# Attention and two mixtures in one kernel: the shifted copy of v made by DMA, and the first expert's weight splits moved off GpSimd

## The chip, the core and the metric

One core of a Trainium2 chip runs the whole program. The metric is the device time of one execution in microseconds (us). Before the change three runs took 689.7, 691.38 and 685.89 us; their median is 689.7 us. One further execution was profiled, and all rows below come from it; its span is 693.8 us. The engines are TensorE (PE; PEld is its weight load), VectorE (DVE), ScalarE (ACT), GpSimd (POOL) and SyncE (SP), which in this program issues the transfers.

## What is computed

Three stages follow each other: windowed attention, a dense mixture of 4 experts over all tokens, and a routed mixture of 8 experts. Only the first two matter for the change.

```python
# attention: q, k, v of (2, 8, 576, 64); a query sees the 64 positions up to its own
scores = scale * np.matmul(q, k.transpose(0, 1, 3, 2))
mask = (rel >= 0) & (rel < window)
attn = softmax(np.where(mask, scores, -1e9))
x = np.matmul(attn, v)              # becomes 1152 tokens of 512
# dense mixture, 4 experts
for e in range(E):
    h = np.maximum(x @ w1[e], 0.0)  # 512 -> 1024
    out += p[:, e:e + 1] * (h @ w2[e])
# routed mixture, 8 experts, one for each token: follows on out
```

## The kernel before, in words

**Precision.** Every large product is made of three matmuls: each operand is split in a high part (a rounded copy) and a low part (the rest). A piece of expert weights is loaded as 512 KB into one of four `raw` buffers (`w_load`, L317 for w1, L319 for w2). `w_split` then makes the high part (L333, a cast) and the low part (L337, a subtraction). Each of w1 and w2 of an expert has four such pieces, c = 0 to 3. A `raw` buffer is free for the next load when the low part of its piece is done.

**Attention.** There are 18 units u of 64 queries, two in each tile t of 128 tokens. `at_s` makes a unit's scores (PE, L415), their maximum (DVE, L428 and L429), the exponentials (ACT, L435), the reciprocal of the sum (DVE, L442 and L443) and the normalised weights `s` (POOL, L446). `at_pv` transposes `s` (PE, L365), copies it out of PSUM to `pT` (ACT, L458; 2 buffers), multiplies with v (PE, L465, "PV" below; one `o` buffer in PSUM) and splits the result into `xth` (ACT, L473) and `xtl` (DVE, L474). The keys of a unit are 128 tokens. For an odd unit they are the tile's own `vn`. For an even unit they are the first half of this tile and the second half of the tile before: the shifted copy `ve` (`mk_ve`, L395 and L398; 2 buffers, while `vn` has 3). The queries and keys are transposed by `at_q` and `at_k` (PE, L365).

**Dense mixture.** `gemm1_chunk` (L525) makes 128 columns of h for a group of tokens; group 0 of the first expert holds 256 tokens and needs `xth` and `xtl` of units 0 to 3 and all of w1. `gemm2_tile` (L546) needs w2. PE may start on these while attention is still going on, and does so.

**Order.** The program is written as operations with an engine, a planned duration, what they read and write, and a priority. A list scheduler (`Plan.run`) turns them into one fixed order for each engine before anything runs; each engine then works through its list and stops at the first instruction whose inputs are missing. SP has such a list too: a `dma_start` that has to wait holds back all transfers behind it. The table `KN` holds priorities and choices: `w1pool`, `w1hpool` and `w2pool` say for each of the four pieces of the first expert whether POOL makes the low part of w1, the high part of w1 and the low part of w2.

Of the kernel before, what the change touches and what calls it, by code (L numbers as in the profile page):

```python
# [15 lines left out]
PSUM = bass.MemoryType.PSUM  # L16
# [13 lines left out]
RP, RH = ((1, 3), (2, 1), (2, 3)), ((1, 2), (2, 2))  # L30
KN = {'mpe': [1, 1, 1, 1, 1, 1, 1, 0, 0, 0, 0, 0, 0, 0, 0, 0, 0, 0], 'UT': 37.5, 'ULATE': -12.9, 'w1p': [3.5, 16.0, 16.5, 20.5], 'w1pool': [1, 0, 0, 0], 'w1hpool': [1, 0, 0, 1], 'ld': [-20.0, -15.9, 3.5, 0.0, -0.9, 4.0], 'w1ld': [-12.5, 2.4, 7.3, 6.7], 'ldb': 0.3, 'lds': 2.4, 'ldv': 65.5, 'qd': [0, 1, 1, 0, 1, 0, 1, 1, 0], 'w2p': 37.8, 'w2s': 18.7, 'w2pool': [1, 1, 0, 0], 'sl': 0.4, 'oq': -38.3, 'ok': -29.0, 'ove': -5.4, 'opv': -6.5, 'dpp': 22.8, 'wpool': [0, 0, 0, 0, 0, 0, 0, 0]}
NU = NT // 64
KC = DM // 128
# [16 lines left out]

# [1 line left out]
class Ring:  # L52
    """a tile tag with n buffers"""

# [11 lines left out]
class Buf:  # L66
    """one use of a ring's buffer; it gets its tile when its first op is emitted"""

# [25 lines left out]
class Plan:  # L94
# [6 lines left out]
    def add(self, eng, dur, fn, rd=(), wr=(), prio=0.0, new=None, slack=0.0):  # L101
        """fn emits; rd and wr are keys (or Bufs) read and written; new: Bufs that get their tile here"""
        o = Op()
        o.slack = slack
        o.eng, o.dur, o.fn, o.prio, o.seq, o.acq = eng, dur, fn, prio, len(self.ops), list(new or ())
        wr = list(wr) + o.acq
        deps = set()
        for x in rd:
            if x in self.w:
                deps.add(self.w[x])  # L110
        for x in wr:
            if x in self.w:
                deps.add(self.w[x])
            deps.update(self.r.get(x, ()))
        for x in rd:
            self.r.setdefault(x, []).append(o)
        for x in wr:
            self.w[x] = o
            self.r[x] = []
        deps.discard(o)  # L120
        o.deps, o.outs, o.wait = deps, [], len(deps)
        for d in deps:
            d.outs.append(o)
        o.bufs = [x for x in dict.fromkeys(list(rd) + wr) if isinstance(x, Buf)]
        for x in o.bufs:
            x.left += 1
        self.ops.append(o)
        return o
# [78 lines left out]
def fused_kernel(ctx: ExitStack, tc: tile.TileContext, q, k, v, dp, w1, w2, wskip, wgate, m1, m2, out):  # L207
# [58 lines left out]
    add = plan.add  # L266

# [1 line left out]
    def c_ident():  # L269
# [26 lines left out]
    def warm(i):  # L296
# [5 lines left out]
        rd=["ident"], wr=["psum1"], prio=-9)  # L302
# [7 lines left out]

# [1 line left out]
    def w_load(src, part, c, prio, extra=False, early=False):  # L312
# [35 lines left out]

# [1 line left out]
    qn, kn, vn, ve, su = {}, {}, {}, {}, {}  # L350
# [41 lines left out]
    def mk_ve(t, pr):  # L392
        w, a = ve_r.buf(), vn[t]
        ve[t] = w
        add("DVE", 0.33, lambda: DVE.tensor_copy(w[0:64], a[0:64]), rd=[a], new=[w], prio=pr)  # L395
        if t:
            c = vn[t - 1]
            add("DVE", 0.33, lambda: DVE.tensor_copy(w[64:128], c[64:128]), rd=[c], wr=[w], prio=pr)  # L398
            c.close()
        else:  # L400
            add("POOL", 0.46, lambda: POOL.memset(w[64:128], 0.0), wr=[w], prio=pr)
# [108 lines left out]

# [1 line left out]
    seq = [0]  # L512
# [49 lines left out]

# [1 line left out]
    R = {"rpr": Ring(None, 3, [128, 128], F32, "rp")}  # L564
# [62 lines left out]
    def route(t):  # L627
# [108 lines left out]
        def spread(c0, c1, pr, after=()):  # L736
            """columns c0 to c1 of w (0, 1: the token's number; 2 to 4: its gate) to the table of slots"""
            e0, n = c0 * E2, (c1 - c0) * E2
# [85 lines left out]

# [1 line left out]
    rings = [{}, wa]  # L826
# [41 lines left out]
    def xsplit(ps, pr):  # L868
        """ps: PSUM buffers that hold KC chunks between them"""
        x, w = M["xs"].buf(), KC // len(ps)  # L870
# [12 lines left out]
    def block(e, j, xg, x, small=False):  # L883
        """up to 128 rows of one expert; small: up to 64 rows, high and low parts side by side in one stationary"""
        ring, key = rings[e], rkey[e % 2]
# [7 lines left out]
        def gemm(name, ps, c, groups, g0=0, g1=None):  # L893
            """groups: list of (operand, its keys, weights, chunks, column slice)"""
            for n, (op, keys, ws, ks, cols) in list(enumerate(groups))[g0:g1]:
# [89 lines left out]

# [1 line left out]
    npass = [0]  # L987
# [19 lines left out]
    with tc.manual_schedule():  # L1007
# [47 lines left out]
        def over(e, i):  # L1055
            """more than 64 * i rows for expert e"""
            return (nv[0] & (7 * 8 ** e)) > (i - 1) * 8 ** e

        def tail(e, j, xt):
            """expert e's rows from 128 * j on, of which there is at least one"""  # L1060
            x = xgs[e, j]
# [93 lines left out]
```

## Time and profile before

| | before |
|---|---|
| runs, median (lowest to highest) | 689.7 us (685.89 to 691.38) |
| span of the profiled execution | 693.8 us |
| PE busy | 641.8 us (93%) |
| DVE busy | 343.1 us (49%) |
| ACT busy | 225.7 us (33%) |
| POOL busy | 140.2 us (20%) |
| mean granted TensorE clock | 0.961 |

Busy time is the union of an engine's instructions; a share of the whole span is a mean over stages that have different limits. Attention takes about the first 95 us, the dense mixture lasts to about 480 us, the routed one to the end. The granted clock 1.00 is 2.4 GHz, 0.50 is 1.2 GHz. The profiled execution is 4.1 us longer than the median of the runs.

### The profile page before, as it was taken

The page shows a single profiled execution, that of the slowest core. Times are in us where ns is not written, and L with a number is a line of the kernel's source. Part 1 is how long each engine was busy: PE and PEld are TensorE (multiplying, and loading weights), DVE is VectorE, ACT ScalarE, POOL GpSimd, SP SyncE. Part 2 cuts the span into 40 slices and gives each one's busy share as a digit, 9 for nine tenths or more (in the row PEclk, how much of TensorE's full clock was granted, in tenths as well). Part 3 has the DMA queues.
Part 4 walks back from the last instruction along what each step waited for, and adds up shares of the span by engine and source line. Part 5 has one row for each costly group of instructions (what it writes and reads, how often), then busy time and mean ns, then how long its engine had stood idle before and what let it go on. Part 6 is the DMA issues. An engine that isn't in the chain of part 4 may idle for free. (4 is left out here: it accounts for less than half of the span.)

```text
span 693.8 us, 9629 instructions
## 1 busy us (share of the span) xinstructions
PE 641.8 (93%) x3652; PEld 563.5 (81%) x3652; DVE 343.1 (49%) x688; ACT 225.7 (33%) x480; POOL 140.2 (20%) x129
## 2 busy tenths in 40 slices
PE   6889999999999999999999999999879888999754
PEld 5788899898989989898989898898758666778543
DVE  5996922147212144121244262657457648937931
ACT  4964731035101133110134121135216524525500
POOL 6550320000000000000000000006047617625610
PEclk9999999999999999999999999999689989999977
DMA  9767000019000034000034110117176664853500
GB/s 216 154 166 225 17 3 1 0 47 296 22 1 1 0 98 146 0 1 1 1 121 122 43 49 32 61 50 265 61 251 224 219 229 131 282 189 101 183 19 12
DMA packets 55372, 70.13 MB, mean 101 GB/s; under 512 B 32857, under 2 KB 32857, under 8 KB 55296
## 3 DMA queue, kind: packets, MB, share of 16 engines
q1 hardware_dynamic: 52912, 62.17, 28.9%
q0 software_dynamic: 2384, 6.97, 3.4%
q8 instruction: 44, 0.72, 0.4%
q14 instruction: 32, 0.26, 0.1%
HBM read 62.43 MB, written 7.47 MB: 101 GB/s over the span
## 5 line engine op out<-in xcount | busy, mean ns | idle before, releaser
L525 PE MATMUL mm<-xth,wa1h 128*128 128x384 f32 (+1 forms) x416 | 137.8, 331 | 0.0
L525 PE MATMUL mm<-xtl,wa1h 128*128 128x384 f32 (+1 forms) x416 | 135.7, 326 | 0.0
L525 PE MATMUL mm<-xth,wa1l 128*128 128x384 f32 (+1 forms) x416 | 135.7, 326 | 0.0
L531 ACT ACTIVATE hh<-mm 128x384 fp32r<-128x384 f32 (+1 forms) x104 | 48.5, 466 | 235.7 <-PE mm L525 227.1
L546 PE MATMUL mm<-wa2h,hh 128*128 128x512 f32 (+1 forms) x296 | 117.2, 396 | 0.0
L533 DVE SCALAR_TENSOR_TENSOR hl<-mm,hh 128x384 fp32r<-128x384 f32 (+1 forms) x104 | 54.5, 525 | 122.9 <-ACT hh L531 122.9
L546 PE MATMUL mm<-wa2h,hl 128*128 128x512 f32 (+1 forms) x296 | 115.0, 388 | 0.0
L546 PE MATMUL mm<-wa2l,hh 128*128 128x512 f32 (+1 forms) x296 | 115.0, 388 | 0.0
L525 PEld LDWEIGHTS mm<-xth,wa1h 128*128 128x128 f32 x416 | 78.7, 189 | 0.7
L525 PEld LDWEIGHTS mm<-xtl,wa1h 128*128 128x128 f32 x416 | 78.7, 189 | 0.5
L525 PEld LDWEIGHTS mm<-xth,wa1l 128*128 128x128 f32 x416 | 78.6, 189 | 0.0
L768 POOL DMA_INDIRECT x<-scr,id x1 | 1.3, 1252 | 360.2 <-DVE id L785 360.2
L546 PEld LDWEIGHTS mm<-wa2h,hl 128*128 128x128 f32 x296 | 55.8, 188 | 12.4
L558 DVE SCALAR_TENSOR_TENSOR x<-mm,prob,x 128x512 f32<-128x512 f32 (+1 forms) x28 | 20.5, 731 | 91.2 <-PE mm L546 91.2
L546 PEld LDWEIGHTS mm<-wa2l,hh 128*128 128x128 f32 x296 | 56.0, 189 | 11.0
L546 PEld LDWEIGHTS mm<-wa2h,hh 128*128 128x128 f32 x296 | 55.9, 189 | 11.1
L337 DVE TENSOR_TENSOR wa2l<-raw,wa2h 128x1024 fp32r<-128x1024 f32 x22 | 40.2, 1837 | 4.9 <-ACT wa2h L333 4.7
L333 ACT CAST wa2h<-raw 128x1024 fp32r<-128x1024 f32 x29 | 30.3, 1047 | 21.8 <-PE mm L546 19.4
L333 ACT CAST wa1h<-raw 128x1024 fp32r<-128x1024 f32 x27 | 27.0, 1049 | 22.5 <-PEq L1109 11.0
L337 DVE TENSOR_TENSOR wa1l<-raw,wa1h 128x1024 fp32r<-128x1024 f32 x25 | 31.6, 1306 | 1.3 <-ACT wa1h L333 1.1
L899 PE MATMUL mm<-wb1h,xs 128*128 128x512 f32 x64 | 25.1, 466 | 7.7 <-PEq L1109 6.8
L947 DVE SCALAR_TENSOR_TENSOR ht<-pt,ht 128x512 fp32r<-128x512 f32 (+2 forms) x27 | 15.1, 567 | 32.8 <-ACT ht L944 31.2
(209 smaller groups left out, 1003.9 us busy)
## 6 DMA issues: line engine op xcount, KB each, us to landing
raw<-in_moe_w_dram SPq DMA_DIRECT2D x96, 512.0 KB, 5.0
scr<-x SPq DMA_DIRECT2D x9, 256.0 KB, 2.1
out_dram<-x SPq DMA_DIRECT2D x9, 256.0 KB, 2.3
qn<-in_q_dram SPq DMA_DIRECT2D x8, 256.0 KB, 4.6
kn<-in_k_dram SPq DMA_DIRECT2D x8, 256.0 KB, 4.1
vn<-in_v_dram SPq DMA_DIRECT2D x8, 256.0 KB, 4.8
qn<-in_q_dram SPq DMA_DIRECT2D x2, 128.0 KB, 4.6
kn<-in_k_dram SPq DMA_DIRECT2D x2, 128.0 KB, 4.7
```

The lines of the kernel that those rows point to most:

```text
L333: (POOL.tensor_copy if hpool else DVE.tensor_copy if hdve else ACT.copy)(out=aps()[0], in_=b.tile)
L337: (POOL if pool else DVE).tensor_tensor(out=l, in0=b.tile, in1=f32(h), op=ALU.subtract)
L525: PE.matmul(out=ps[:, 0:n], lhsT=wa[a][:, kk, f * 128:(f + 1) * 128], rhs=x[:, kk, g0:g0 + n], start=(i == 0), stop=(i == 3 * KC - 1))
L531: add("ACT", c_act(n), lambda: ACT.activation(out=hh[:, f, 0:n], in_=ps[:, 0:n], func=ACTF.Relu), rd=[ps], wr=[("hh", f)], prio=-1)
L533: add("DVE", c_dve(n), lambda: DVE.scalar_tensor_tensor(out=hl[:, f, 0:n], in0=ps[:, 0:n], scalar=0.0, in1=f32(hh[:, f, 0:n]), op0=ALU.max ...
L546: PE.matmul(out=ps[:, 0:c1 - c0], lhsT=x[:, f, o:o + 128], rhs=wa[a][:, f, c0:c1], start=(f == 0 and i == 0), stop=(f == FC - 1 and i == 2))
L558: DVE.scalar_tensor_tensor(out=z, in0=y, scalar=prob[:, t, e:e + 1], in1=z, op0=ALU.mult, op1=ALU.add)
L768: add("POOL", 1.0, lambda: POOL.indirect_dma_start(out=R["x0"], out_offset=None, in_=scr[0:128 * (GT + 1), :], in_offset=bass.IndirectOffs ...
L899: PE.matmul(out=ps[:, 0:cols.stop - cols.start], lhsT=op(k), rhs=ring[f"{c}{a}"][:, k, cols], start=(n == 0 and k == ks[0] and a == "h"), ...
L947: add("DVE", c_dve(w * n), lambda: DVE.scalar_tensor_tensor(out=ht[:, s, n:2 * n], in0=p[:, 0:w, 0:n], scalar=0.0, in1=f32(ht[:, s, 0:n]), ...
```

## The change

Two things are edited. The entries `w1pool`, `w1hpool` and `w2pool` of the first expert become all zero: the high parts of w1's pieces 0 and 3 go from POOL to ACT, the low part of piece 0 of w1 and of pieces 0 and 1 of w2 from POOL to DVE. And `mk_ve` copies the two halves of `ve` by `dma_start` on SP, from SBUF to SBUF, where DVE copied before: 9 copies at L395 and 8 at L398, each of 64 partitions by 512 values (128 KB). The rest of the diff takes comments away.

```diff
-KN = {'mpe': [1, 1, 1, 1, 1, 1, 1, 0, 0, 0, 0, 0, 0, 0, 0, 0, 0, 0], 'UT': 37.5, 'ULATE': -12.9, 'w1p': [3.5, 16.0, 16.5, 20.5], 'w1pool': [1, 0, 0, 0], 'w1hpool': [1, 0, 0, 1], 'ld': [-20.0, -15.9, 3.5, 0.0, -0.9, 4.0], 'w1ld': [-12.5, 2.4, 7.3, 6.7], 'ldb': 0.3, 'lds': 2.4, 'ldv': 65.5, 'qd': [0, 1, 1, 0, 1, 0, 1, 1, 0], 'w2p': 37.8, 'w2s': 18.7, 'w2pool': [1, 1, 0, 0], 'sl': 0.4, 'oq': -38.3, 'ok': -29.0, 'ove': -5.4, 'opv': -6.5, 'dpp': 22.8, 'wpool': [0, 0, 0, 0, 0, 0, 0, 0]}
+KN = {'mpe': [1, 1, 1, 1, 1, 1, 1, 0, 0, 0, 0, 0, 0, 0, 0, 0, 0, 0], 'UT': 37.5, 'ULATE': -12.9, 'w1p': [3.5, 16.0, 16.5, 20.5], 'w1pool': [0, 0, 0, 0], 'w1hpool': [0, 0, 0, 0], 'ld': [-20.0, -15.9, 3.5, 0.0, -0.9, 4.0], 'w1ld': [-12.5, 2.4, 7.3, 6.7], 'ldb': 0.3, 'lds': 2.4, 'ldv': 65.5, 'qd': [0, 1, 1, 0, 1, 0, 1, 1, 0], 'w2p': 37.8, 'w2s': 18.7, 'w2pool': [0, 0, 0, 0], 'sl': 0.4, 'oq': -38.3, 'ok': -29.0, 'ove': -5.4, 'opv': -6.5, 'dpp': 22.8, 'wpool': [0, 0, 0, 0, 0, 0, 0, 0]}
...
     def mk_ve(t, pr):
         w, a = ve_r.buf(), vn[t]
         ve[t] = w
-        add("DVE", 0.33, lambda: DVE.tensor_copy(w[0:64], a[0:64]), rd=[a], new=[w], prio=pr)
+        add("SP", 0.4, lambda: SP.dma_start(out=w[0:64], in_=a[0:64]), rd=[a], new=[w], prio=pr)
         if t:
             c = vn[t - 1]
-            add("DVE", 0.33, lambda: DVE.tensor_copy(w[64:128], c[64:128]), rd=[c], wr=[w], prio=pr)
+            add("SP", 0.4, lambda: SP.dma_start(out=w[64:128], in_=c[64:128]), rd=[c], wr=[w], prio=pr)
             c.close()
```

Since the scheduler plans with other engines and durations, it writes another order for attention on every engine. Three places are shown. The number behind a name tells the buffers apart; in brackets stands what an instruction waits for (DMAHW0 to DMAHW7 are the counters that SP's transfers use in turn).

SP, from the load of q's tile 7 on. Before (`qn_534` is q's tile 7, `raw_584` the first piece of w2, `vn_631` v's tile 2):

```order
L354 DMA qn_534<-in_q_dram 128x8x64 [waits DMAHW2_49,PE_49]
L354 DMA kn_547<-in_k_dram 128x8x64 [waits DMAHW3_49,PE_49]
L507 DMA prob_100<-in_moe_domain_probs_dram 128x9x4 [waits DMAHW0_49]
L319 DMA raw_584<-in_moe_w2_dram 128x2x512 [waits DMAHW1_49,Pool_49]
L319 DMA raw_608<-in_moe_w2_dram 128x2x512 [waits DVE_49]
L354 DMA vn_631<-in_v_dram 128x8x64
L354 DMA vn_655<-in_v_dram 128x8x64 [waits DMAHW4_49,DVE_49]
L319 DMA raw_676<-in_moe_w2_dram 128x2x512 [waits DMAHW5_49,DVE_49]
```

And now (`qn_504` is q's tile 7, `raw_525`, `raw_540`, `raw_551` and `raw_556` are the four pieces of w2, `vn_284`, `vn_306` and `vn_546` v's tiles 0 to 2, `ve_554` the shifted copy for unit 2, `ve_559` that for unit 4, `raw_562` the first piece of the second expert's w1):

```order
L354 DMA qn_504<-in_q_dram 128x8x64 [waits DMAHW3_49,PE_49]
L507 DMA prob_100<-in_moe_domain_probs_dram 128x9x4
L319 DMA raw_525<-in_moe_w2_dram 128x2x512 [waits DMAHW1_49,DVE_49]
L319 DMA raw_540<-in_moe_w2_dram 128x2x512 [waits DMAHW2_49,DVE_49]
L354 DMA vn_546<-in_v_dram 128x8x64
L319 DMA raw_551<-in_moe_w2_dram 128x2x512 [waits DMAHW4_49,DVE_49]
L395 DMA ve_554<-vn_306 64x512 [waits DMAHW5_49]
L319 DMA raw_556<-in_moe_w2_dram 128x2x512 [waits DMAHW6_49,DVE_49]
L395 DMA ve_559<-vn_546 64x512 [waits DMAHW7_49,DMAHW3_49,Pool_49]
L317 DMA raw_562<-in_moe_w1_dram 128x1024 [waits DMAHW1_49,DMAHW0_49,DVE_49]
L398 DMA ve_554<-vn_284 64x512
```

The second half of unit 2's copy now stands on SP behind `ve_559`, which waits for v's tile 2 to land, and behind `raw_562`, which takes the buffer of `raw_525` and so waits until DVE has made the low part of that piece.

PE, from the transposes of unit 4 to the first matmul of the dense mixture. Before (`sp_465` and `sp_499` are the scores of units 8 and 9, `o_477` is the PV of unit 3, `qn_449` q's tile 5, `kn_462` k's tile 5; the PV of units 0 and 2 are done by then):

```order
L365 MATMUL pt_457<-ident_93,s_364 128x128 x4
L415 MATMUL sp_465<-kt0_114,qz0_112 128x128 x4
L465 MATMUL o_477<-pT_453,vn_310 64x64 x8
L365 MATMUL pt_493<-ident_93,qn_449 128x128 x4
L415 MATMUL sp_499<-kt0_114,qz0_112 128x128 x4
L365 MATMUL pt_509<-ident_93,kn_462 128x128 x4
L525 MATMUL mm_519<-xth_106,wa1h_108 128x256
```

And now (`s_363`, `s_393`, `s_451` and `s_456` are units 4 to 7, `sp_466` and `sp_474` the scores of units 8 and 9, `o_442`, `o_569` and `o_590` the PV of units 3, 2 and 5, `qn_432` is q's tile 5):

```order
L365 MATMUL pt_436<-ident_93,s_363 128x128 x4
L465 MATMUL o_442<-pT_420,vn_306 64x64 x8
L365 MATMUL pt_460<-ident_93,s_393 128x128 x4
L415 MATMUL sp_466<-kt0_114,qz0_112 128x128 x4
L415 MATMUL sp_474<-kt0_114,qz0_112 128x128 x4
L365 MATMUL pt_493<-ident_93,qn_432 128x128 x4
L365 MATMUL pt_513<-ident_93,s_451 128x128 x4
L465 MATMUL o_569<-pT_355,ve_554 64x64 x8
L365 MATMUL pt_583<-ident_93,s_456 128x128 x4
L465 MATMUL o_590<-pT_580,vn_546 64x64 x8
L525 MATMUL mm_601<-xth_106,wa1h_108 128x256
```

The PV of unit 2, with its shifted copy `ve_554`, has moved behind q's tile 5. Ahead of the dense mixture there now stand three more transposes (units 5, 6 and 7) and one more PV (unit 5), and k's tile 5 comes later; ahead of q's tile 5 there stand one more unit's scores and one more transpose, and one PV fewer.

ACT, behind the exponentials of unit 9 (`s_518` is unit 9; `pt_460` is the transposed unit 5, `o_569` the result of unit 2's PV). Before, ACT's casts of w2 stood one at a time between outputs of the dense mixture (L531):

```order
L333 CAST wa2h_110<-raw_584 128x1024 [waits DMAHW1_49]
L531 ACTIVATE hh_104<-mm_612 128x256 [waits PE_49]
L333 CAST wa2h_110<-raw_608 128x1024 [waits DMAHW2_49]
L531 ACTIVATE hh_104<-mm_635 128x256 [waits PE_49]
L531 ACTIVATE hh_104<-mm_657 128x256 [waits PE_49]
```

And now:

```order
L435 ACTIVATE s_518,mx_527<-s_518,mx_527 128x128 x3
L333 CAST wa2h_110<-raw_525 128x1024 [waits DMAHW1_49]
L333 CAST wa2h_110<-raw_540 128x1024 [waits DMAHW2_49]
L333 CAST wa2h_110<-raw_551 128x1024 [waits DMAHW4_49]
L333 CAST wa2h_110<-raw_556 128x1024 [waits DMAHW6_49]
L458 COPY pT_580<-pt_460 128x512 [waits PE_49]
L473 CAST xth_106<-o_569 128x4x64
```

All four casts of w2 now stand together, ahead of unit 5's `pT` and unit 2's `xth`. On DVE the four low parts of w2 (L337) stand together in the same way, ahead of unit 2's `xtl`.

## Rows read from the trace of the kernel before

**Rows 1.** Busy time by stretch; columns: stretch, length, busy of each engine, clock, DMA, GB/s.
```profile
20.00:30.00 10.00, 7.90 (x94) 6.92 (x94) 8.84 (x24) 8.68 (x40) 5.52 (x6) 1.00 0.78 196
30.00:34.16 4.16, 3.81 (x45) 3.65 (x45) 4.09 (x8) 3.95 (x13) 1.04 (x1) 1.00 0.10 23
34.16:50.70 16.54, 14.29 (x131) 13.78 (x129) 15.63 (x38) 11.88 (x39) 7.82 (x5) 1.00 0.68 166
50.70:480.00 429.30, 429.23 (x2472) 386.36 (x2473) 170.90 (x414) 114.37 (x241) 20.29 (x40) 1.00 0.20 63
```

**Rows 2.** Instructions in order of time: the one long PE wait; columns: start, length, instruction.
```profile
43.26 4.74 POOL L337 TENSOR_TENSOR wa2l<-raw,wa2h 128x1024 fp32r<-128x1024 f32 x2
45.92 2.36 DVE L395 COPY ve<-vn 64x512 f32<-64x512 f32 x1
50.71 0.51 PE L465 MATMUL o<-pT,ve 128*64 128x64 f32 x10 [2.26 <-DVE xtl L474]
```

**Rows 3.** Busy time in two stretches at half clock, columns as in rows 1.
```profile
52.06:55.40 3.34, 3.34 (x17) 3.28 (x16) 2.38 (x5) 1.25 (x6) 0.00 (x0) 0.50 1.07 318
514.80:519.70 4.90, 4.88 (x12) 3.88 (x13) 0.00 (x0) 0.00 (x0) 0.00 (x0) 0.50 0.98 306
```

**Rows 4.** Instructions of PE in order of time, 30 to 34.2 us.
```profile
30.35 0.63 PE L365 MATMUL pt<-ident,s 128*128 128x128 f32 x4 [1.47 <-ACT pT L458]
30.82 1.06 PE L415 MATMUL sp<-kt,qz 128*128 128x128 f32 x8
31.80 0.68 PE L465 MATMUL o<-pT,vn 128*64 128x64 f32 x16
32.42 0.66 PE L365 MATMUL pt<-ident,qn 128*128 128x128 f32 x4
...
33.80 0.60 PE L365 MATMUL pt<-ident,kn 128*128 128x128 f32 x4
34.16 0.36 PE L525 MATMUL mm<-xth,wa1h 128*128 128x256 f32 x1
```

**Rows 5.** Transfers that SP issues, in order of time; columns: start, length of issue, transfer.
```profile
33.10 0.37 SPq L354 DMA_DIRECT2D qn<-in_q_dram  x1
34.43 0.37 SPq L354 DMA_DIRECT2D kn<-in_k_dram  x1
34.85 0.58 SPq L507 DMA_DIRECT2D prob<-in_moe_domain_probs_dram  x1
35.52 1.51 SPq L319 DMA_DIRECT2D raw<-in_moe_w_dram  x2
```

**Rows 6.** Issues with KB and us to landing, at 34.85, 35.52, 37.08, 38.27; last: whole span.
```profile
prob<-in_moe_domain_probs_dram SPq DMA_DIRECT2D x1, 18.0 KB, 3.2
raw<-in_moe_w_dram SPq DMA_DIRECT2D x1, 512.0 KB, 4.2
vn<-in_v_dram SPq DMA_DIRECT2D x1, 256.0 KB, 5.3
raw<-in_moe_w_dram SPq DMA_DIRECT2D x1, 512.0 KB, 6.6
scr<-x SPq DMA_DIRECT2D x9, 256.0 KB, 2.1
```

**Rows 7.** Groups of instructions, 0 to 100 us; columns: busy us, mean ns, idle before.
```profile
L333 ACT CAST wa2h<-raw 128x1024 fp32r<-128x1024 f32 x4 | 4.2, 1038 | 0.0
L337 DVE TENSOR_TENSOR wa2l<-raw,wa2h 128x1024 fp32r<-128x1024 f32 x2 | 2.4, 1224 | 0.1
L398 DVE COPY ve<-vn 64x512 f32<-64x512 f32 x8 | 3.4, 424 | 0.2
L458 ACT COPY pT<-pt 128x512 f32<-128x512 f32 x18 | 10.6, 587 | 3.8 <-PE o L465 2.8 <-PE pt L365 0.8
L473 ACT CAST xth<-o 128x256 fp32r<-128x256 f32 x18 | 6.7, 371 | 5.8 <-PE o L465 5.7
L474 DVE TENSOR_TENSOR xtl<-o,xth 128x256 fp32r<-128x256 f32 x18 | 7.5, 415 | 1.5 <-ACT xth L473 1.4
```

## Prediction

> **What bounds the kernel now.** I read the busy time by stretch first. From 50.7 us to 480 us PE is busy for 429.23 of 429.30 us, in the three stretches from 20 us up to there it is idle for 2.10, 0.35 and 2.25 us, and the first matmul of the dense mixture starts at 34.16 us [rows 1]. So until 480 us PE does its list without a gap, and whatever PE loses in the first 50 us comes out at the end one for one. Attention decides how much that is: DVE is busy for 8.84 of 10 us, 4.09 of 4.16 and 15.63 of 16.54 us in the three stretches from 20 us on [rows 1], ahead of PE in none of them by much, and the order on each engine is fixed.
>
> Next I looked for PE's idle time in the timeline. The 2.25 us of the stretch from 34.16 us are one wait of 2.26 us for unit 5's `xtl` [rows 2]. On DVE that `xtl` stood behind copies of `ve`, one of which took 2.36 us while POOL was making two low parts of w2 for 4.74 us [rows 2]; the second copies are 0.42 us long on average [rows 7]. A little after this idle time the granted clock fell to 0.50, that is 1.2 GHz, from 52.06 to 55.40 us, PE busy all along [rows 3]: 3.34 us in which half the work was done, 1.67 us lost. The change removes just these two things, the copies from DVE and the splits from POOL. At most 2.25 + 1.67 = 3.9 us are to be had from it there.
>
> Then I read how SP behaves. q's tile 7 was issued at 33.10 us, when PE had finished transposing tile 5 (32.42 + 0.66) [rows 4, 5]. k's tile 7 came at 34.43 us, right after PE had transposed k's tile 5 (33.80 + 0.60) [rows 4, 5], and `prob` and two pieces of w2 followed at 34.85 and 35.52 us [rows 5], though nothing that they need was late. A transfer that waits on SP holds back those behind it.
>
> **The change part by part.** *Removed from DVE*: 17 copies of some 0.42 us [rows 7], 7 us over attention. *Added to DVE*: three low parts at 1.22 us [rows 7], 3.7 us. *Added to ACT*: two casts of about 1.04 us [rows 7]. In sum DVE has 3 us less to do; it is not what I expect to end last, so I price these at nothing apart from the 3.9 us above. The first cast and low part of w1 fall in the first 10 us, where ACT and DVE wait for PE in any case; if that cover failed it would cost 1 to 2 us.
>
> *The 17 copies on SP, and the new order.* Let t0 be the moment when q's tile 5 has been transposed; 33.08 us before. By the order printed above PE now has one more unit's scores (0.98 us from row to row), one more transpose (0.47) and one PV fewer (0.62) ahead of it [rows 4]: 0.83 us more, t0 = 33.9, if PE's idle time up to there stays; 31.5 if all 2.45 us of idle between 20 and 34.16 us [rows 1] vanish with the lighter DVE. DVE has only 0.8 to 1.2 us less to do up to there (two or three copies), so I take 33.4.
>
> From t0 on, with the spacing of issues seen before (0.42 us behind q or k, 0.67 behind `prob`, 0.75 for a piece of w2 [rows 5]; for v and a half of `ve` I estimate 0.4 to 0.5 from the 0.37 of q): `prob` at t0 + 0.4, w2's pieces 0 and 1 at + 1.1 and + 1.9, v's tile 2 at + 2.6, piece 2 at + 3.1, the first half of `ve_554` at + 3.9, piece 3 at + 4.3. Now `ve_559` waits for v's tile 2: 2.6 + 5.3 [rows 6] = 7.9. Behind it `raw_562` waits for the low part of piece 0: landed at 1.1 + 4.2 [rows 6] = 5.3, cast 1.04 and low part 1.22 [rows 7], 7.6. So `raw_562` is issued at t0 + 8.3 and the second half of `ve_554` only at t0 + 9.1.
>
> How long a copy within SBUF takes no row shows. From below: a 256 KB store that has the queue to itself lands after 2.1 us [rows 6]; t0 + 11.2. From above: it lands behind everything ahead of it. Piece 3 lands by 4.3 + 6.6 = 10.9, and `raw_562` 4.2 to about 6 us [rows 6] after its issue; t0 + 12.5 to 14.5. `prob`, with its 18 KB, took 3.2 us behind k's tile, longer than the 256 KB store alone [rows 6]; so I lean to the upper end and take t0 + 13. The Trainium skill's page "DMA: Bandwidth & Descriptors", section "Queues, rings and completion order", says that each DMA engine consumes the descriptors of one queue in ring order, though a later one may complete earlier. By that rule the copy starts behind `raw_562` and the sum is the one taken; with the 2.1 us alone it would be 1.8 us less. The row on `prob` agrees with it.
>
> The PV of unit 2 starts then, and nothing on PE's list can be done meanwhile but one transpose. Behind it: PV 0.68 us [rows 4], `pT` of unit 5 0.59, `xth` 0.37, `xtl` 0.42 [rows 7], the PV of unit 5 0.68, some 0.4 us for five hand-overs (an estimate from the gaps between such rows): 3.1 us. The dense mixture starts at t0 + 16.1 = 49.5 us.
>
> The same start is held back a second time. ACT has all four casts of w2 ahead of that `pT` and `xth`, and DVE all four low parts ahead of `xtl`. Piece 3 lands at t0 + 10.9; cast 1.04, low part 1.22, `xtl` 0.42, the PV of unit 5 0.68: t0 + 14.3 with no copy late at all. If `ve` came in time, this would be late next.
>
> **The sum**, against the profiled execution. The start of the dense mixture moves from 34.16 to 49.5 us, 15.3 us. Of that, three transposes and a PV less k's transpose (3 x 0.47 + 0.62 - 0.4, about 1.6 us [rows 4]) are work that PE no longer has to do later: 13.7 us lost. The old wait and its slow clock are given back: -3.9. A PE idle for over 10 us comes back at half clock: after the idle time ahead of 514.80 us it was at 0.50 for 4.90 us [rows 3], so +2.4. Behind that PE has some 40 us of work in attention and group 0 and DVE some 30, so I add 1 us of further waits (0 to 4): each v tile has to wait for a `ve` half to land before its buffer is free, and each `ve` for a v tile. 13.7 - 3.9 + 2.4 + 1 = 13.2 us: 707.0 us for a profiled execution like this one, which lies 4.1 us above the median of the runs; against the median 689.7, **702.9 us**. Low end: t0 = 31.5, copy at + 11.2, no further waits: 8.5 us, 698.2. High end: t0 = 33.9, copy at + 14.5, 4 us of waits: 18.2 us, 707.9.
>
> **The rivals.** *Faster: the copies arrive in time.* If SP reached the second half of `ve_554` before PE needs it, and w2 landed before ACT needs it, PE would keep its 34 us start and the 3.9 us would be won: 685.8 us. The copy of 2.36 us beside POOL's 4.74 us [rows 2] speaks for it; so does the Trainium skill's page "SBUF — State Buffer", section "Who interferes with whom": VectorE and GpSimd share a port pair as an exclusive lock, the later one blocks. The length of the copy agrees: it ended with POOL's work. Against it stands the order on SP and ACT. It decides from a start of the dense mixture at about 38 us on: 4 us late, less 1.6 us of work moved, plus 1.2 to 2.4 us of slow clock, eat the 3.9. I see no way to load, cast and split four pieces between 33.4 and 38 us. 5 in 100.
>
> *Held back but not long.* If w2's pieces landed after 4.2 us each rather than 6.6, and the copy after 2.1, and t0 was 31.5, the start would be at 43 to 44 us: 6 to 7 us lost net, 696 us, about within 1%. The rows of 5.3 and 6.6 us, from just this place in the program [rows 6], speak against it. 10 in 100.
>
> *Attention goes on at the pace of SP.* Each later tile needs v (5.3 us), then `ve` (2.1 to 4 us), before the buffer of v is free for the next but two. If PE waited for that at units 6, 8 and 10, 2 us each, or at more, the time would be 709 to 713 us. By my reckoning PE is about 1 us behind the copies there. 12 in 100.
>
> **How the numbers follow.** The likeliest case, 73 in 100, gives 702.9 with 698 to 708. To leave out no more than 2 in 10 the range reaches from 696.5 to 709. A measurement of this kernel tells about 1% from no change, 682.8 to 696.6: faster 0.04, same 0.09, slower 0.87.
>
> **What would show it.** In the profile after: the first L525 at 46 to 51 us instead of 34.16; ahead of it a PE wait of 8 to 13 us at L465 for a DMA of `ve` (or at L365, for `pT`); SP waiting for `wa2l` with `ve` behind it; clock 0.50 for 4 to 5 us afterwards; the same PE work from there to the end. Wrong it would be with a first L525 before 40 us, or if PE found something to do meanwhile; the size is off if copies land within 2 us behind loads.

## The result and the profile after

The change makes the kernel slower: 697.87 us (696.24 to 700.52) after, 690.54 us (685.89 to 691.84) before in the same comparison, a ratio of 1.0124 with a 95% interval of 1.0075 to 1.0173. That is 7.3 us; the forecast was 13.2 us, 702.9 us in total. The profiled execution after has a span of 694.4 us. A few executions of any kernel take several us longer than its others and are left out of the ratios; the profiled one of the last experiment, e11, is among them (694.0 us against 681.7 to 683.4), so nothing is read from its profile.

| | before | after |
|---|---|---|
| first matmul of the dense mixture | 34.16 us | 49.76 us |
| end of the dense mixture | 486.98 us | 499.67 us |
| from there to the end of the span | 206.8 us | 194.7 us |
| PE busy | 641.8 us | 635.5 us (92%) |
| DVE busy | 343.1 us | 330.3 us (48%) |
| ACT busy | 225.7 us | 227.1 us (33%) |
| POOL busy | 140.2 us | 130.3 us (19%) |

"End of the dense mixture" is here and below the start of PE's first instruction behind its 2.1 us wait for the last `x` (L558), which every one of these kernels has.

The busy time by stretch of the kernel after, to be held against [rows 1] (columns as there):

```profile
20.00:30.00 10.00, 9.57 (x111) 8.43 (x110) 8.67 (x22) 9.81 (x41) 4.50 (x5) 1.00 0.95 228
30.00:34.16 4.16, 1.55 (x14) 1.31 (x13) 4.06 (x11) 3.36 (x13) 1.15 (x2) 1.00 0.37 67
34.16:49.76 15.60, 3.83 (x41) 3.04 (x41) 9.89 (x18) 8.19 (x23) 3.01 (x3) 0.56 1.02 284
49.76:53.00 3.24, 3.24 (x17) 3.24 (x16) 0.42 (x1) 1.14 (x3) 0.00 (x0) 0.51 0.70 200
53.00:480.00 427.00, 425.56 (x2479) 383.84 (x2478) 161.78 (x390) 110.27 (x246) 13.05 (x37) 1.00 0.17 53
```

From 34.16 to 49.76 us, where PE was busy most of the time before (14.29 of 16.54 us [rows 1]), it now works for 3.83 of 15.60 us. The DMA engines are full there (share 1.02; 0.68 before in about the same stretch). PE comes back at half clock, 0.51 until 53 us. From there to 480 us it loses 1.44 us in all, in one wait for DVE's `mx`.

The instructions of PE in that stretch, in order of time (start, length, instruction; in brackets PE's idle time ahead of it and its releaser, which is the instruction whose end PE waited for):

```profile
30.95 0.60 PE L365 MATMUL pt<-ident,qn 128*128 128x128 f32 x4
34.44 0.63 PE L365 MATMUL pt<-ident,s 128*128 128x128 f32 x4 [2.89 <-ACT qz L375]
45.80 1.12 PE L465 MATMUL o<-pT,ve 128*64 128x64 f32 x16 [10.73 <-DMA ve<-vn]
47.69 1.09 PE L365 MATMUL pt<-ident,s 128*128 128x128 f32 x4 [0.77 <-ACT pT L458]
48.70 1.12 PE L465 MATMUL o<-pT,vn 128*64 128x64 f32 x16
49.76 0.58 PE L525 MATMUL mm<-xth,wa1h 128*128 128x256 f32 x1
```

PE waits 10.73 us for unit 2's `ve`, the longest wait of the kernel. SP's issues from v's tile 2 on:

```profile
34.11 0.46 SPq L354 DMA_DIRECT2D vn<-in_v_dram  x1
34.66 0.54 SPq L319 DMA_DIRECT2D raw<-in_moe_w_dram  x1
35.25 0.51 SPq L395 DMA_DIRECT2D ve<-vn  x1
35.85 0.54 SPq L319 DMA_DIRECT2D raw<-in_moe_w_dram  x1
39.61 0.51 SPq L395 DMA_DIRECT2D ve<-vn  x1
41.15 0.34 SPq L317 DMA_DIRECT2D raw<-in_moe_w_dram  x1
41.53 0.47 SPq L398 DMA_DIRECT2D ve<-vn  x1
```

and how long the first, third, sixth and seventh of them took from issue to landing (KB, us):

```profile
vn<-in_v_dram SPq DMA_DIRECT2D x1, 256.0 KB, 5.4
ve<-vn SPq DMA_DIRECT2D x1, 128.0 KB, 6.6
raw<-in_moe_w_dram SPq DMA_DIRECT2D x1, 512.0 KB, 4.0
ve<-vn SPq DMA_DIRECT2D x1, 128.0 KB, 4.2
```

SP stops for v's tile 2 (34.11 + 5.4 = 39.5) and for the low part of piece 0 of w2 (41.15), so the second half of unit 2's `ve` goes out at 41.53 and lands at 45.7 us; PE's PV starts at 45.80.

### The profile page after: what moved, and what is told of

Same layout as the page of the kernel before. It is cut to its first block, busy times and chain, and to the rows that moved or that the text cites. A ratio compares the mean times of both kernels' runs of the same rounds, so it can differ in the third digit from the quotient of the medians.

```text
span 694.4 us, 9648 instructions
## 1 busy us (share of the span) xinstructions
PE 635.5 (92%) x3652; PEld 558.9 (80%) x3652; DVE 330.3 (48%) x674; ACT 227.1 (33%) x482; POOL 130.3 (19%) x124
## 5 line engine op out<-in xcount | busy, mean ns | idle before, releaser
L525 PE MATMUL mm<-xth,wa1h 128*128 128x384 f32 (+1 forms) x416 | 138.0, 332 | 0.0
L525 PE MATMUL mm<-xth,wa1l 128*128 128x384 f32 (+1 forms) x416 | 135.6, 326 | 0.0
L525 PE MATMUL mm<-xtl,wa1h 128*128 128x384 f32 (+1 forms) x416 | 135.6, 326 | 0.0
L531 ACT ACTIVATE hh<-mm 128x384 fp32r<-128x384 f32 (+1 forms) x104 | 48.5, 467 | 243.5 <-PE mm L525 234.8
L525 PEld LDWEIGHTS mm<-xth,wa1h 128*128 128x128 f32 x416 | 78.8, 189 | 0.9
L525 PEld LDWEIGHTS mm<-xtl,wa1h 128*128 128x128 f32 x416 | 78.8, 189 | 0.4
L525 PEld LDWEIGHTS mm<-xth,wa1l 128*128 128x128 f32 x416 | 78.7, 189 | 0.0
L546 PEld LDWEIGHTS mm<-wa2h,hl 128*128 128x128 f32 x296 | 55.7, 188 | 12.4
L546 PEld LDWEIGHTS mm<-wa2l,hh 128*128 128x128 f32 x296 | 55.8, 188 | 11.2
L558 DVE SCALAR_TENSOR_TENSOR x<-mm,prob,x 128x512 f32<-128x512 f32 (+1 forms) x28 | 20.5, 731 | 91.2 <-PE mm L546 91.2
L337 DVE TENSOR_TENSOR wa2l<-raw,wa2h 128x1024 fp32r<-128x1024 f32 x24 | 38.2, 1603 | 6.4 <-ACT wa2h L333 6.4
L333 ACT CAST wa1h<-raw 128x1024 fp32r<-128x1024 f32 x29 | 29.1, 1049 | 21.7 <-PEq L1109 10.3
L337 DVE TENSOR_TENSOR wa1l<-raw,wa1h 128x1024 fp32r<-128x1024 f32 x26 | 33.4, 1322 | 2.4 <-ACT wa1h L333 2.4
L899 PE MATMUL mm<-wa1h,xs 128*128 128x512 f32 (+1 forms) x60 | 22.6, 437 | 9.2 <-issue 6.3
```

What stands on the lines that cost most here:

```text
L333: (POOL.tensor_copy if hpool else DVE.tensor_copy if hdve else ACT.copy)(out=aps()[0], in_=b.tile)
L337: (POOL if pool else DVE).tensor_tensor(out=l, in0=b.tile, in1=f32(h), op=ALU.subtract)
L525: PE.matmul(out=ps[:, 0:n], lhsT=wa[a][:, kk, f * 128:(f + 1) * 128], rhs=x[:, kk, g0:g0 + n], start=(i == 0), stop=(i == 3 * KC - 1))
L531: add("ACT", c_act(n), lambda: ACT.activation(out=hh[:, f, 0:n], in_=ps[:, 0:n], func=ACTF.Relu), rd=[ps], wr=[("hh", f)], prio=-1)
L546: PE.matmul(out=ps[:, 0:c1 - c0], lhsT=x[:, f, o:o + 128], rhs=wa[a][:, f, c0:c1], start=(f == 0 and i == 0), stop=(f == FC - 1 and i == 2))
L558: DVE.scalar_tensor_tensor(out=z, in0=y, scalar=prob[:, t, e:e + 1], in1=z, op0=ALU.mult, op1=ALU.add)
```

## The experiments

Theory: two holdbacks, SP's order for the copy and the order of w2's splits on ACT and DVE for `pT` and `xtl`. Rivals: SP's order alone; ACT's and DVE's order alone; the copies in themselves. In e1 to e3, e5 and e6 the planned lists are edited by hand, instruction by instruction, and PE's and POOL's lists stay those of after; the edits of e1 to e3 and e5 are shown in words, the others as code. All results (us; "dense ends" as defined above; the ratio is to before on the same chip):

| kernel | first dense matmul | dense ends | span profiled | median | ratio, 95% interval |
|---|---|---|---|---|---|
| before | 34.16 | 486.98 | 693.8 | 690.5 | |
| after | 49.76 | 499.67 | 694.4 | 697.9 | 1.0124 (1.0075 to 1.0173) |
| e1 copy moved | 49.64 | 499.73 | 696.0 | 697.7 | 1.0094 (1.0063 to 1.0125) |
| e2 splits moved | 51.06 | 500.29 | 698.0 | 699.8 | 1.0114 (1.0082 to 1.0147) |
| e3 both moved | 46.71 | 497.83 | 696.9 | 699.6 | 1.0110 (1.0025 to 1.0195) |
| e4 before again | 34.02 | 487.53 | 689.2 | 690.3 | 0.9998 (0.9965 to 1.0031) |
| e5 needed first | 41.47 | 493.03 | 690.7 | 693.9 | 1.0022 (0.9982 to 1.0062) |
| e6 ACT's queue | 49.78 | 499.09 | 699.9 | 699.9 | 1.0104 (1.0014 to 1.0194) |
| e7 splits alone | 35.15 | 485.35 | 686.5 | 687.9 | 0.9968 (0.9941 to 0.9995) |
| e8 copies alone | 52.25 | 504.41 | 700.4 | 703.0 | 1.0168 (1.0090 to 1.0246) |
| e9 before, no POOL | 34.28 | 487.24 | 683.1 | 682.6 | 0.9884 (0.9844 to 0.9924) |
| e10 after, no POOL | 52.04 | 502.07 | 696.8 | 698.5 | 1.0142 (1.0096 to 1.0188) |
| e11 splits, no POOL | not read | not read | not read | 683.3 | 0.9904 (0.9867 to 0.9941) |

**e1: the copy moved up on SP.**

```diff
 SP: ve_554<-vn_306, first half of unit 2's copy
+SP: ve_554<-vn_284, its second half
 SP: raw_556, piece 3 of w2
 SP: ve_559<-vn_546, first half of unit 4's copy
 SP: raw_562, piece 0 of the second expert's w1
-SP: ve_554<-vn_284
```

> The kernel after with one transfer moved on SP: the second half of unit 2's `ve` stands right behind its first half, ahead of the fourth piece of w2; every other engine's list is word for word that of after. Theory (two holdbacks): the copy lands some 6 us earlier, at about 39.5 us instead of 45.7, but `pT` of unit 5 stands behind ACT's four casts of w2 and `xtl` of unit 2 behind DVE's four low parts, which end at about 45.5 us as in after; the first matmul of the dense mixture comes at 46.5 to 47.5 us instead of 49.76, and the end of the dense mixture (the 2.1 us wait of PE for the last x, 499.67 us in after) 2 to 3 us earlier. Rival 1 (SP's order alone): first dense matmul at 43 to 44 us, end of the dense mixture 6 us earlier. Rival 2 (a copy within SBUF takes 6 us or more by itself at this place): 48.5 to 49.8 us, end less than 1 us earlier.

PE in order of time, and the landing of the moved copy, issued at 36.01 us:

```profile
44.19 1.12 PE L513 MATMUL o<-pT,ve 128*64 128x64 f32 x16 [8.50 <-DMA ve<-vn]
47.57 1.08 PE L413 MATMUL pt<-ident,s 128*128 128x128 f32 x4 [2.26 <-ACT pT L506]
49.64 0.58 PE L573 MATMUL mm<-xth,wa1h 128*128 128x256 f32 x1
...
ve<-vn SPq DMA_DIRECT2D x1, 128.0 KB, 8.0
```

(Line numbers of e1, e2, e3 and e5 are higher by 48: L513 is L465, L413 L365, L573 L525.) Issued 5.5 us earlier, the copy lands only 1.7 us earlier, at 44.0 us: it takes 8.0 us. I had expected about 3.5 us, so the first dense matmul did not come at 47 us; the second rival named this. The other holdback is there as expected: PE now waits 2.26 us for `pT`, which ACT makes behind the fourth cast. The move itself made this one later: the fourth piece of w2, now behind the copy, landed at 45.8 us instead of 43.2.

**e2: the splits moved.**

```diff
 ACT: casts of w2, pieces 0 and 1
-ACT: casts of w2, pieces 2 and 3
 ACT: pT of unit 5, xth of unit 2
+ACT: casts of w2, pieces 2 and 3
 DVE: low parts of w2, pieces 0 and 1
-DVE: low parts of w2, pieces 2 and 3
 DVE: xtl of unit 2
+DVE: low parts of w2, pieces 2 and 3
```

> The kernel after with four instructions moved: ACT's casts of pieces 2 and 3 of w2 stand behind unit 5's `pT` and unit 2's `xth`, DVE's low parts of these pieces behind unit 2's `xtl`; SP and PE as in after. Theory (two holdbacks, the copy is the later one): first dense matmul at 49.0 to 49.8 us, end of the dense mixture within 0.7 us of after's 499.67. Rival 1 (SP's order alone): the same. Rival 3 (the order on ACT and DVE alone holds PE back, the wait for `ve` only falls together with it): 45 to 47 us, end 3 to 5 us earlier.

No gain: the copy landed at 47.0 us in this execution, 1.3 us later than in after, and PE waited 12.17 us for it; so the first dense matmul came at 51.06 us, later than the 49.0 to 49.8 expected. That ACT's and DVE's order alone holds PE back is refuted.

**e3: both.**

> Both moves in one kernel. Theory (two holdbacks): first dense matmul at 43 to 44 us, end of the dense mixture 5.5 to 6.5 us earlier than in after, that is 3 us more than the move of the copy alone and the move of the splits alone bring together. Rival 1 (SP's order alone): as the move of the copy alone. Rival 3 (ACT and DVE alone): as the move of the splits alone. In total 692 to 694 us by the theory if the routed mixture takes as long as in after's median.

```profile
42.75 1.12 PE L513 MATMUL o<-pT,ve 128*64 128x64 f32 x16 [7.50 <-DMA ve<-vn]
44.64 1.09 PE L413 MATMUL pt<-ident,s 128*128 128x128 f32 x4 [0.77 <-ACT pT L506]
45.65 1.12 PE L513 MATMUL o<-pT,vn 128*64 128x64 f32 x16
46.71 0.58 PE L573 MATMUL mm<-xth,wa1h 128*128 128x256 f32 x1
```

Only together do the moves bring something in these profiles: the dense mixture starts 3.05 us and ends 1.84 us earlier, and PE waits for the copy alone (7.50 us), not for `pT` behind the casts. With the wait of 2.26 us in e1 this shows two holdbacks. The size is less certain than that: e10 below, whose lists up to there are those of after, differs from after by 2.3 us in the same start. The gain is half of what I expected or less, since the copy still takes 6.5 us, and PE then waits 1.40 us for unit 4's `ve`. The total shows nothing of it.

**e4: before once more**, to see how much a profile of the same kernel varies.

> The kernel before, unchanged, for a second profiled execution. In the first one the dense mixture ended (PE's wait for the last x) at 486.98 us and the rest took 206.8 us; in the one of after 499.67 us and 194.7 us, so 12.7 us of delay in attention came out as 0.6 us between these two. Theory: the length of the routed part varies by several us from execution to execution, and before's first profile was a long one: the dense mixture ends at 486.5 to 487.5 us again, the rest takes 198 to 204 us. Rival: before's routed part is always near 206.8 us and a later start takes 12 us from it: 206 to 208 us again.

The dense mixture ends within 0.6 us of the first profile, and the rest takes 201.7 us instead of 206.8: it varies by 5 us. Most of that is the clock at the start of the rest, here in the first profile of before and in e4 (columns as in [rows 1]):

```profile
486.98:499.20 12.22, 11.18 (x42) 9.51 (x43) 4.97 (x33) 2.33 (x6) 0.00 (x0) 0.50 0.12 44
487.53:499.20 11.67, 10.63 (x58) 9.26 (x59) 5.85 (x38) 3.47 (x8) 0.00 (x0) 0.85 0.15 54
```

By the clock the first lost about 6.1 us there and e4 1.8 (an estimate: the length times what is missing to 1.00). In after the clock was 0.86 in this stage, as in e4, so e4 is the profile to compare with. Its rest is still 7.0 us longer than the 194.7 us of after. So a part of the 12 us is really given back in the routed mixture; e9 and e10 look for it.

**e5: what is needed first goes first.**

```diff
 SP: kn, k's tile 6
+SP: ve_554, both halves
 SP: qn_504, q's tile 7
+SP: vn_546, v's tile 2
 SP: prob, w2's pieces 0 to 3
 SP: ve_559, first half
+SP: ve_559, second half; of all later copies too
-ACT: casts of w2 ahead of pT of unit 5 and xth of unit 2
+ACT: casts of w2 behind them; DVE: low parts of w2 behind xtl of unit 2
```

> The kernel after with transfers and splits put in the order in which they are needed; PE's and POOL's lists word for word as in after. On SP both halves of unit 2's `ve` stand ahead of q's tile 7, v's tile 2 right behind q's tile 7, and each later second half of `ve` right behind its first half; on ACT and DVE all casts and low parts of w2 stand behind unit 2's `xth` and `xtl`. Theory (the loss is the order in which SP's queue is served plus the splits ahead of `pT`, and nothing of the copies themselves): no PE wait for unit 2's `ve`; `pT` of unit 5 made at 38.3 to 39 us, first dense matmul at 39.5 to 41.5 us instead of 49.76, end of the dense mixture 488 to 491 us instead of 499.67, within 3 us of before's 487. With a rest of 195 to 202 us: 685 to 695 us, not slower than before by more than 0.5 per cent. Rival (the copies cost in themselves, since each takes its turn on the same 16 DMA engines as the loads): later units wait for `ve` instead, end of the dense mixture at 494 us or more.

```profile
34.68 0.63 PE L413 MATMUL pt<-ident,s 128*128 128x128 f32 x4 [2.88 <-ACT qz L423]
35.24 0.98 PE L513 MATMUL o<-pT,ve 128*64 128x64 f32 x16
39.40 1.09 PE L413 MATMUL pt<-ident,s 128*128 128x128 f32 x4 [3.18 <-ACT pT L506]
41.47 0.58 PE L573 MATMUL mm<-xth,wa1h 128*128 128x256 f32 x1
```

The copy goes out at 27.17 and 27.80 us, and the wait for it is gone. The dense mixture starts 8.3 us and ends 6.6 us earlier than in after, 2 us later than I had hoped and 1 us short of the rival's 494. What stays is mostly PE's own list: with three more units' transposes and unit 5's PV ahead it waits 2.88 us for `qz` and 3.18 us for `pT` behind ACT's exponentials; for a later `ve` it waits 0.85 us. In total e5 can't be told from before, though its dense mixture ends 5.5 to 6.1 us later: like after, it doesn't have the wait in the routed mixture that e9 takes up.

**e6: the two transfers of unit 2's copy issued by ACT.**

```diff
-SP.dma_start(out=w[0:64], in_=a[0:64])    # unit 2 only, and the second half
+ACT.dma_start(out=w[0:64], in_=a[0:64])   # behind the exponentials of unit 8
```

> The kernel after with the two transfers of unit 2's `ve` issued by ACT, behind the exponentials of unit 8, instead of by SP; all else in its order. In the run with the copy moved up on SP they took 8.0 and 8.2 us from issue to landing, behind two pieces of w2 and v's tile 2. Theory 1 (a queue is served in order, so the copies waited behind the loads of their own queue): from ACT's queue they land within 2 to 4 us of their issue, at 38 to 39.5 us; then the splits ahead of `pT` and `xtl` are the later holdback, first dense matmul at 46.5 to 48 us. Theory 2 (the 16 DMA engines are full, whatever the queue): 6 to 8 us again, landing at 42 to 44 us, first dense matmul at 47.5 to 49.7 us.

Issued at 35.53 and 36.09 us. The landing of the fourth piece of w2, issued by SP at the same time, and of the two copies:

```profile
raw<-in_moe_w_dram SPq DMA_DIRECT2D x1, 512.0 KB, 10.5
ve<-vn ACTq DMA_DIRECT2D x2, 128.0 KB, 7.7
```

Another queue helps nothing: the first copy takes 6.9 us, the second 8.5, and PE's PV starts at 44.70 us. The DMA share was 1.06 from the first issue to there. The piece of w2 takes 10.5 us, where it took 7.3 in after. So it is not the place in SP's queue that makes a copy slow here; that fits the second theory, that the DMA engines are full. Where the share fell to 0.58 within the time of the copy, in e5, it took 3.6 to 3.7 us. The Trainium skill's page "DMA: Bandwidth & Descriptors", section "Issuing engines are not separate DMA queues", says that transfers of all issuing engines run on the same 16 DMA engines and interleave; the 7.7 us agree.

**e7 and e8: each part alone.** e7 is the kernel before with only the new `KN`, e8 the kernel before with only the new `mk_ve`.

> One part of the change alone: the splits of the first expert on ACT and DVE, `ve` copied by DVE as before. In its order ACT's casts of w2 stand one at a time between outputs of the dense mixture, and the first dense matmul comes behind one more pair of transposes of q and k than in before. Theory: this part costs next to nothing; first dense matmul at 34 to 38 us, PE idle for 5 to 10 us in the first 70 us as in before, end of the dense mixture 485.5 to 488.5 us; total within 1 per cent of before, between 685 and 694 us. Rival (DVE with 3.7 us of low parts more becomes the limit of attention): end of the dense mixture at 491 us or more.

> The other part alone: `ve` by transfers on SP, the splits as before (POOL makes the low parts of pieces 0 and 1 of w2). Its order on SP, PE and ACT has the same pattern as after: the second half of unit 2's `ve` behind a load that waits for a low part, all four casts of w2 ahead of `pT`. Theory: all of the loss is here; first dense matmul at 48.5 to 51.5 us, end of the dense mixture 498.5 to 501.5 us, total 695 to 701 us. Rival (the splits' move from POOL to DVE and ACT holds PE back): first dense matmul before 42 us, end of the dense mixture before 492 us.

The splits alone are a small gain: the dense mixture ends 1.6 to 2.2 us earlier, the median is 0.3% lower and the interval stays just below 1. The copies alone lose 1.7%, no less than both parts together: all of the loss is theirs, in the order that the scheduler gives with them (e5 has the same 17 copies in another). e8 came out later than I had expected throughout: 52.25 us, 504.41 us and 703.0 us in total. Their wait in e8:

```profile
48.28 1.12 PE L465 MATMUL o<-pT,ve 128*64 128x64 f32 x16 [10.08 <-DMA ve<-vn]
52.25 0.58 PE L525 MATMUL mm<-xth,wa1h 128*128 128x256 f32 x1
```

**e9, e10, e11: what the routed mixture gives back.** In it POOL makes some low parts. In e4, POOL, DVE and PE while the fourth expert's weights are split:

```profile
544.56 2.40 POOL L337 TENSOR_TENSOR wa1l<-raw,wa1h 128x1024 fp32r<-128x1024 f32 x1
...
545.50 7.19 DVE L337 TENSOR_TENSOR wa2l<-raw,wa2h 128x1024 fp32r<-128x1024 f32 x1
546.91 4.68 POOL L337 TENSOR_TENSOR wa2l<-raw,wa2h 128x1024 fp32r<-128x1024 f32 x2
...
553.94 1.11 PE L365 MATMUL pt<-ident,xg 128*128 128x128 f32 x4 [5.10 <-DVE xs L878]
```

and in the kernel after the same instructions:

```profile
554.12 0.40 PE L899 MATMUL mm<-wb1l,xs 128*128 128x512 f32 x1 [1.45 <-issue]
...
556.50 2.41 POOL L337 TENSOR_TENSOR wa1l<-raw,wa1h 128x1024 fp32r<-128x1024 f32 x1
...
559.06 1.22 DVE L337 TENSOR_TENSOR wa2l<-raw,wa2h 128x1024 fp32r<-128x1024 f32 x1
...
560.31 2.83 POOL L337 TENSOR_TENSOR wa2l<-raw,wa2h 128x1024 fp32r<-128x1024 f32 x1 [1.41 <-ACT wa2h L333]
```

In e4 DVE starts its low part while POOL is at one, and gets on only when POOL has made two more: it ends 1.1 us after the last of them, 7.19 us after its start; `xs` stands behind it and PE waits 5.10 us. In after PE lost 1.45 us a little earlier, DVE comes 0.15 us after POOL has ended, and its low part takes 1.22 us. Behind the wait PE is at half clock in e4, and not in after, whose clock is 1.00 here (columns as in [rows 1]):

```profile
553.94:559.66 5.72, 5.72 (x16) 4.66 (x17) 2.37 (x3) 0.63 (x1) 0.00 (x0) 0.50 0.98 361
554.12:566.00 11.88, 11.88 (x60) 9.84 (x60) 8.29 (x10) 6.25 (x9) 9.49 (x5) 1.00 0.64 228
```

So the collision costs e4 5.10 us and half of 5.72 us more, 8.0 in all; after lost 1.45 us in its place. The difference, 6.5 us, is nearly all of the 7.0 us by which e4's rest is longer. The 5.1 us occur in before, e4 and e7, in no profile with `ve` by transfer. The edit of e9 (on before), e10 (on after) and e11 (on e7) gives POOL's three low parts to DVE:

```diff
-kd == "r" and ((p, c) in RP if e > 1 else ...
+kd == "r" and ((p, c) in RP and e != 3 if e > 1 else ...
```

> The kernel before with one edit in the routed mixture: the three low parts of the fourth expert's weights that POOL makes are made by DVE. In both profiles of before, PE waits 5.1 us for DVE's `xs` there, while one low part on DVE lasts 7.2 us beside two on POOL; in all profiles with `ve` by transfer PE first loses 0.9 to 1.5 us at another place (for no releaser that shows), DVE's low part then fits ahead of POOL's two, and the 5.1 us don't occur. Theory: they are what the routed mixture gives back of the 12 to 13 us. Then here the wait goes (under 2 us left), the rest behind the dense mixture takes 195 to 199 us instead of 201.7, the total falls by 3 to 5 us to 685 to 688 us. Rival (the wait is for a late transfer, or DVE is the limit there whatever POOL does): the wait stays at 4 us or more, total as before within 1.5 us.

> The kernel after with the same edit in the routed mixture. Theory: nothing is to be had here, since after had no such wait: 695 to 700 us, within 2 us of after's 697.9; so against the edited kernel before the change now costs 10 to 13 us instead of 7.3, about as much as the 12.1 to 12.7 us by which the dense mixture ends later. Rival (the routed mixture gives the time back by another way): the difference of the edited kernels stays at 6 to 8 us.

> A version that may beat both kernels: the splits of the first expert on ACT and DVE (687.9 us in their own run), `ve` copied by DVE as before, and the edit in the routed mixture. Theory: both gains add, since one ends the dense mixture 2 us earlier and the other takes the 5.1 us wait away: 682 to 685.5 us, 0.6 to 1.1 per cent faster than before. Rival (no gain from the edit): 686.5 to 689 us.

In e9 the wait is gone, and the clock is 1.00 from 540 to 570 us; DVE's low parts there take 1.22 us each:

```profile
548.33 1.22 DVE L337 TENSOR_TENSOR wa1l<-raw,wa1h 128x1024 fp32r<-128x1024 f32 x1
...
550.09 0.69 DVE L878 TENSOR_TENSOR xs<-pt,xs 128x512 fp32r<-128x512 f32 x1
```

Before gains 7.4 us by the edit (689.98 to 682.56), more than the 3 to 5 expected, which left out the slow clock behind the wait; after gains nothing (698.5). Between the edited kernels the change costs 15.9 us, more than the 10 to 13 expected, and their dense mixtures end 14.8 us apart. Of these 14.8, e10's profile has 2.4 more than after's by itself: with the same lists up to there it waited 12.79 us for unit 2's `ve` instead of 10.73. So one profile tells this delay to 2 or 3 us only. Within that, the routed mixture gave the time back by this one collision, which before has and after misses; why PE loses the 1.45 us ahead of it stays open. e9, at 682.6 us, and e11, at 683.3 us, beat both kernels. e11 lies in the range expected of it, but it is no faster than e9: that the splits' gain of e7 adds to that of e9 is not shown.

## Why the prediction was right, and where it was off

The direction, the place and the mechanism up to the end of the dense mixture were right, and 697.9 us lies in the range; the size was 5 us too high. By its steps:

- **t0.** Taken 33.4 us (31.5 to 33.9); 31.55 us (30.95 + 0.60). Nearly all of PE's idle time ahead of it was gone: 9.57 us busy from 20 to 30 us instead of 7.90 [rows 1]. The lighter DVE, by which I had bounded this, is not needed for it: in e7, where DVE copies as before and has the low parts too, PE is busy for 9.59 of these 10 us. I had also taken the copies on DVE at 7 us; the nine at L395 take 676 ns on average, so it is 9.5.
- **SP's order.** v's tile 2 landed at t0 + 8.0 (forecast 7.9). `raw_562` went out at t0 + 9.6 instead of 8.3: ACT was still at unit 9's exponentials when piece 0 landed and cast it only from 38.30 us on.
- **The copy.** It landed at t0 + 14.2 (forecast 13, bounds 11.2 to 14.5), 4.2 us after its issue and just behind `raw_562`. The value was right, the reason not wholly: I leaned on the order within one queue, as the Trainium skill's page "DMA: Bandwidth & Descriptors", section "Queues, rings and completion order", has it. The landings in after come in the order of issue, which agrees; but e6 shows that the wait is as long from another queue.
- **The chain to the first dense matmul.** 3.96 us instead of 3.1, because PE is at half clock in it (PV 1.12 us instead of 0.68 [rows 4]); I had put the slow clock only behind it. This (+0.9), the copy (+1.2) and the early t0 (-1.9) nearly cancel: 49.76 us, forecast 49.5. That it came so close is luck.
- **The second holdback.** The last low part of w2 was put at t0 + 13.2 (10.9 + 1.04 + 1.22); it ended at 45.5 us, t0 + 14.0. e1 and e3 show that it would be late next.
- **Given back** were the old wait and its slow clock, as forecast [rows 2, 3]. The new slow clock behind the start cost 1.6 us (3.24 us at 0.51) instead of 2.4, further waits 1.4 instead of 1. The sum up to the end of the dense mixture is 13.2 us in the forecast; measured are 12.7 us against the first profile of before and 12.1 against e4 (e10 in place of after: about 2.4 more).
- **The step that failed** is in the first paragraph: "whatever PE loses in the first 50 us comes out at the end one for one". It comes out at the end of the dense mixture. Behind it stands the routed mixture, a list with waits of its own, which I had not priced; that only the first two stages matter for the change, as I wrote at the start, was wrong. Of 12.4 us (the mean of 12.1 and 12.7) 7.3 are left by the medians, so 5.1 us are given back there. The profiles show where: after misses a collision of 8.0 us (the wait of 5.1 us and the half clock behind it) and loses 1.45 us instead. Without the collision (e9, e10) one for one about holds: 14.8 us by the profiles and 15.9 by the medians.
- **The rivals on the slow side** did not come: the start is at 49.8 us and not at 43 to 44, and attention does not go on at the pace of SP, with one further wait of 1.44 us up to 480 us, and that for DVE. The first of them was also mispriced: its own conditions (t0 = 31.5, the second half of `ve_554` issued at + 9.1 and landed after 2.1, a chain of 3.1) give a start at 45.8 us, the low end of the likeliest case, or some 45 with v's tile in 4.2 us, not 43 to 44.
- **The rival that ended faster** rested on the row in which a copy took 2.36 us beside POOL [rows 2] and on the Trainium skill's page "SBUF — State Buffer", section "Who interferes with whom", an exclusive lock between VectorE and GpSimd. In attention this gain exists but is small (e7: 690.12 to 687.92 us in one comparison). In the routed mixture, which the change doesn't touch, a collision of the same two engines is worth 7.4 us (e9); the rows of 7.19 and 1.22 us agree with the page, which doesn't say that one blocked instruction may wait for three.

## What to carry to other kernels

A copy moved to a DMA queue costs nothing on the engine that it leaves, but it now waits for whatever that queue waits for, and for the DMA engines' load: look at their busy share at that place, and issue the copy ahead of bulk loads that nobody needs yet. A delay reaches the end of a program only through every later stage; look there too for waits that depend on which of two engines comes first. Such a collision can hide half of a loss, or be worth as much as the change under study.

## What the runs showed of the hardware

- A low part on DVE that met a running one on POOL waited for that one and two more that followed on POOL: 7.19 us for 1.22 us of work. DVE got no turn between POOL's instructions. PE's wait of 5.10 us behind it was followed by 5.72 us at 0.50.
- Copies of 128 KB within SBUF landed 4.2 to 8.5 us after their issue while the DMA share was about 1 (1.04 to 1.08), from either queue, and a load of 512 KB beside them took longer (9.1 us in e1 and 10.5 in e6 instead of 7.3). Their median over the whole kernel after is 3.1 us.
- After a wait of 10.73 us PE ran at 0.50 from 45.8 to 52.9 us, 7.1 us; before, 4.9 us after a wait of 4.0 [rows 3].
- In each profile with `ve` by transfer PE lost 0.9 to 1.5 us at one and the same matmul of the third routed expert, for no releaser that the profile shows, and in none of the others (1.45 us in after, 1.08 in e10). The cause stays open.
